# A chunked state-space scan feeding a cosine-gated two-layer network: the scan cut into twelve 64-token units instead of six 128-token chunks

## The chip, the core and the metric

One core of a Trainium2 chip runs the whole program. The metric is the device time of one execution in microseconds (us). The kernel before was timed in three runs. One further execution was recorded by the hardware profiler, and all rows below come from that one. The engines are TensorE (PE in the profile, its weight loads PEld), VectorE (DVE), ScalarE (ACT), GpSimd (POOL) and SyncE (SP, which here only issues transfers).

## What is computed

There are two stages. The first is a scan over 768 tokens, for 4 sequences of 8 heads, with a state of 16 by 32 for each head. The second multiplies the 3072 rows of 256 numbers with `w_in`, gates with `h * cos(h)` and multiplies with `w_out`.

```python
# scan: x (4, 8, 768, 32), a (4, 8, 768), B and C (4, 8, 768, 16); chunk = 32
cum = np.cumsum(la, axis=-1)                       # la = log(clip(a)) of one chunk
L = np.exp(cum[:, :, :, None] - cum[:, :, None, :]) * causal
M = np.einsum('bhin,bhjn->bhij', Cc, Bc) * L
y_intra = np.einsum('bhij,bhjd->bhid', M, xc)
y_inter = np.einsum('bhin,bhnd->bhid', Cc, state) * np.exp(cum)[:, :, :, None]
y[:, :, sl] = y_intra + y_inter
Bx = np.einsum('bhjn,bhjd->bhjnd', Bc, xc) * decay_from_j[:, :, :, None, None]
state = decay_full[:, :, None, None] * state + np.sum(Bx, axis=2)
# network on the 3072 x 256 rows: w_in 256 x 2048, w_out 2048 x 256
h = x @ w_in
out = (h * np.cos(h)) @ w_out
```

The chunk length is free, because the recurrence gives the same result for any cut. The weights come as 64-bit numbers and are turned into 32-bit ones on the chip.

## The kernel before

**Steps of the network.** The main loop (lines 827 to 884) has 96 steps, 16 for each of six chunks of 128 tokens. A step takes 256 rows (the tokens of two sequences) and one eighth of the 2048 columns. `first(n)` (line 568) multiplies four times on TensorE into the PSUM tile `hp` (line 578); ScalarE makes the integer turn `k` (line 582), VectorE the remainder `w` (line 584), ScalarE the sine (line 589) and VectorE the gated product `gT` (line 594). `second(n)` runs two steps later on TensorE: four multiplications in the first 16 steps (line 637) and seven smaller ones after that (line 675), for which GpSimd prepares differences `gd` (lines 619 to 622). The order of TensorE in a step is therefore hp of step n, then o of step n-2, then, after some steps, a piece of the scan.

**Weights.** `w_in` and `w_out` arrive in eight pieces each (`fetch`, line 197). Each piece is converted by `grade` (ScalarE line 222 and 220, GpSimd line 223) and `join` (VectorE lines 236 and 238, GpSimd line 246). The dictionary `piece` (line 768) says in which step a piece is joined: at an odd step n piece (n+3)/2 of `w_in`, at an even step n piece n/2 of `w_out`. With `turn_of` (line 563) the steps 2j and 2j+1 of chunk 0 use piece j of both. `join` of step n stands on VectorE between `w` and `gT` of that step.

**Scan of a chunk.** Tokens lie on the 128 partitions, one sequence at a time. `decays` (line 372) makes the decay matrix `lam` with a running product on VectorE (line 378), `intra2` (line 463) multiplies C and B on TensorE in tiles of 32 rows by 64 columns of the array (line 474), `masked` (line 480) multiplies the two on VectorE (line 495), and `finish2` (line 499) adds on TensorE the share of the old state (line 509, tiles of 32 by 64), the share of the chunk itself (line 516, tiles of 128 by 32) and the new state (line 537, same tiles). From chunk 2 on, B and C are also fetched in 32-token blocks (`load_blocks`, line 135), which VectorE transposes (line 438). TensorE visits the scan three times per chunk: `intra2` for sequences 0 and 1, `intra2` for 2 and 3, and `finish2` for all four. PSUM has two buffers of two banks for it (`pair`, line 89).

**Start.** Chunk 0 is computed before step 0, except for sequence 3, whose last part stands after hp of step 0 (`first_scan`, line 786). Two filling multiplications (line 730) keep TensorE going from the start while inputs arrive. Transfers are issued by SP in program order (`load` line 127, `fetch` line 197, and so on); a transfer waits for the eighth transfer before it.

Of the kernel before, what the change touches and what calls it, by code (L numbers as in the profile page):

```python
# [25 lines left out]
def kernel(  # L26
# [10 lines left out]

# [11 lines left out]
    HH = H // 2  # L67
# [3 lines left out]
    W = P // 2  # L71

    const = ctx.enter_context(tc.tile_pool(name="const", bufs=1))
    loads = ctx.enter_context(tc.tile_pool(name="loads", bufs=2))
    rows = ctx.enter_context(tc.tile_pool(name="rows", bufs=NB))
# [4 lines left out]
    two = ctx.enter_context(tc.tile_pool(name="two", bufs=2))  # L80
# [8 lines left out]
    def pair(name):  # L89

        return psum.tile([P, 2, 4 * P], FP32, tag="scan", bufs=2, name=name)


    raw, arow, along, blocks = {}, {}, {}, {}
# [9 lines left out]

# [3 lines left out]
    def load(c, seqs=(0, NB), only=(B, C, x)):  # L108

        if c >= NC:  # L110
            return
        if c not in raw:
            raw[c] = (loads.tile([P, 2, NB * H, N], FP32, tag="bc", name="bc"),
                      loads.tile([P, NB, H, D], FP32, tag="xr", name="xr"))
        bc, xr = raw[c]
        xr = xr.rearrange("p b h d -> p (b h) d")
        for dst, src in ((bc[:, 0], B), (bc[:, 1], C), (xr, x))[::2 if c > 1 else 1]:

            if not any(src is o for o in only):
                continue  # L120
            halves = c > 0 and src is not C
            for b in range(*seqs) if halves else seqs[:1]:
                rs = slice(b * H, (b + 1 if halves else seqs[1]) * H)
                for t in range(2 if halves and b % 2 else 1):
                    n = W if halves and b % 2 else P
                    ts = slice((n - t * W) % P, (n - t * W) % P + n)
                    nc.sync.dma_start(  # L127
                        out=dst[ts, rs], in_=src[b:b + 1 if halves else seqs[1], :,
                                                 c * P + t * W:c * P + t * W + n, :]
                        .rearrange("b h s n -> s (b h) n"))  # L130

    def by_blocks(c, u):
        return c > 1

    def load_blocks(c, u):

        blocks[c, u] = to_ = loads.tile([P, 2, 2, 4, 2, N], FP32, tag="blocks", name="blocks")  # L140
        for s in range(2):
            for k, src in enumerate((B, C)):
                of = src[2 * u + s, :, c * P:(c + 1) * P].rearrange(
                    "(q h) (m t) n -> m h q t n", h=2, t=32)
                for m in range(4):
                    for h in range(2):
                        nc.sync.dma_start(out=to_[:, k, s, (m + 2 * s) % 4 if k == 0 else m, h],
                                          in_=of[m, h])
                        yield

    def load_a(c, seqs=range(NB)):
        if c >= NC:
            return
        for b in seqs:
            arow[c, b] = t = rows.tile([P, H, P], FP32, tag="arow", name="arow")
            nc.sync.dma_start(
                out=t, in_=a_cut[b, :, c * P:(c + 1) * P].unsqueeze(0).to_broadcast([P, H, P]))

    def load_along(c, seqs=range(NB)):

        if c >= NC:
            return
        if c not in along:
            along[c] = rows.tile([P, NB, P], FP32, tag="along", bufs=2, name="along")
        for b in seqs:
            nc.sync.dma_start(
                out=along[c][:, b], in_=a_all[b, :, c * P:(c + 1) * P].unsqueeze(1)
                .to_broadcast([H, N, P]))


    a0 = const.tile([P, P], FP32, name="a0")
    a0z = const.tile([P, P], FP32, name="a0z")
    nc.sync.dma_start(out=a0[0:NB * H], in_=a[:, :, 0:P].rearrange("b h p -> (b h) p"))
    for r in (slice(NB * H, W), slice(W, P)):
        V.memset(a0[r], 1.0)
# [34 lines left out]

# [19 lines left out]
    def join(which, i):  # L230

        parts = held.pop((which, i), ())
        for e, (high, bits, last) in enumerate(parts):
# [12 lines left out]
    for b in range(NB):  # L248
        if b == NB - 1:
            fetch("in", 0)  # L250
        load(0, (b, b + 1))
    nc.sync.dma_start(
        out=a_in, in_=a.rearrange("(u b) h (c p) -> (b h c) u p", u=NU, p=P))
    for w in (("in", 1), ("out", 0), ("in", 2), ("out", 1), ("in", 3)):
        fetch(*w)
# [5 lines left out]
    V.memset(quarter, HALF_PI)  # L261


    unit = const.tile([P, HH * P + W], FP32, name="unit")
    G.tensor_copy(out=unit[:, 0:HH * P].rearrange("p (h i) -> p h i", h=HH),
                  in_=ident.unsqueeze(1).to_broadcast([P, HH, P]))


    ms = [scan.tile([P, 2 * H * W], FP32, tag=f"m{b}", bufs=1, name="m") for b in range(NB)]
    m_of = [t.rearrange("p (e h i) -> p e h i", e=2, h=H) for t in ms]  # L270
    m_at = [t.rearrange("p (h i) -> p h i", h=H) for t in ms]
    unit0, tos = m_of[NB - 1][:, 0], m_of[NB - 1][:, 1]
    for t in range(2):
        ts = slice(t * W, (t + 1) * W)
        V.tensor_copy(out=unit0[ts], in_=ident[ts, ts].unsqueeze(1).to_broadcast([W, H, W]))

    slot = const.tile([P, 2], FP32, name="slot")
    mine = const.tile([P, H], FP32, name="mine")
    those = const.tile([P, NB], FP32, name="those")
    bh = ident[:, 0:NB * H]  # L280
# [5 lines left out]
    ACT.activation(const.tile([P, 1], FP32, name="sine"), quarter, AF.Sin)  # L286


# [3 lines left out]
    V.tensor_scalar(out=a0, in0=a0, **clip)  # L292


    to = const.tile([P, W], FP32, name="to")
    V.tensor_tensor_scan(out=to, data0=a0[:, W:P], data1=ones[:, 0:W], initial=1.0,
                         op0=ALU.mult, op1=ALU.mult)
    fro = const.tile([P, W], FP32, name="fro")
    V.memset(fro, 1.0)
    V.tensor_tensor_scan(out=fro[:, W - 2::-1], data0=a0[:, W - 1:0:-1],  # L300
                         data1=ones[:, 0:W - 1], initial=1.0, op0=ALU.mult, op1=ALU.mult)
    fros = const.tile([P, NB, W], FP32, name="fros")
    V.tensor_tensor(out=fros, in0=fro.unsqueeze(1).to_broadcast([P, NB, W]),
                    in1=those.unsqueeze(2).to_broadcast([P, NB, W]), op=ALU.mult)
    V.tensor_reduce(out=slot, in_=ident.rearrange("p (k t n) -> p t k n", t=2, n=N),
                    axis=mybir.AxisListType.XY, op=ALU.add)


    a0s = m_of[NB - 2]
    halves = a0z.rearrange("p (t i) -> p t i", t=2)  # L310
    for h in range(HH):
        ACT.activation(a0s[:, :, h], halves, AF.Copy, scale=mine[:, h:h + 1])
# [5 lines left out]


    scaled, lam, reach, state, part, yT = {}, {}, {}, {}, {}, {}  # L320

    def heads(b):
        return slice(b * H, (b + 1) * H)

# [104 lines left out]

    turned = {}

    def turn_blocks(c, u):
# [479 lines left out]
```

## Time and profile before

| what | value |
|---|---|
| median of three runs | 377.41 us |
| lowest and highest | 376.71 and 377.42 us |
| span of the profiled execution, first to last instruction | 374.9 us |
| busy: TensorE, VectorE, GpSimd, ScalarE | 367.1, 286.0, 215.1, 176.0 us |
| matmul records on TensorE | 3108 |
| start of hp of step 0, 1 and 2 | 17.81, 21.16 and 23.32 us |
| start of the first o (step 0's second product) | 25.71 us |
| end of the last o | 371.2 us |
| spacing of hp and of o, first 16 steps | 1.73 and 1.73 us |
| spacing of hp and of o, later steps | 1.73 and 1.56 us |

The span leaves out 2.5 us of the median. The profiled execution has no time of its own besides the span. A multiplication of 32-bit numbers appears as two matmul records with a weight load each. TensorE's records overlap and their ends are modelled, so the spacing from one start to the next is read, not the duration. A line of the timeline gives start, duration, engine, source line, operation, destination and source tile, shape and count, and in brackets the idle time before it and what ended it.

### The profile page before, as it was taken

The page shows a single profiled execution, that of the slowest core. Times are in us where ns is not written, and L with a number is a line of the kernel's source. Part 1 is how long each engine was busy: PE and PEld are TensorE (multiplying, and loading weights), DVE is VectorE, ACT ScalarE, POOL GpSimd, SP SyncE. Part 2 cuts the span into 40 slices and gives each one's busy share as a digit, 9 for nine tenths or more (in the row PEclk, how much of TensorE's full clock was granted, in tenths as well). Part 3 has the DMA queues.
Part 4 walks back from the last instruction along what each step waited for, and adds up shares of the span by engine and source line. Part 5 has one row for each costly group of instructions (what it writes and reads, how often), then busy time and mean ns, then how long its engine had stood idle before and what let it go on. Part 6 is the DMA issues. An engine that isn't in the chain of part 4 may idle for free.

```text
span 374.9 us, 8382 instructions
## 1 busy us (share of the span) xinstructions
PE 367.1 (98%) x3108; PEld 325.4 (87%) x3108; DVE 286.0 (76%) x478; ACT 176.0 (47%) x304; POOL 215.1 (57%) x335
## 2 busy tenths in 40 slices
PE   8999999999999999999999999999999999999996
PEld 3478888889899899999899998999999989999995
DVE  8879999889799957987767987766887872554543
ACT  3887666544344434344334445434444443443442
POOL 6767555589946346665354693353775344444451
PEclk9999999999999999999999999999999999999999
DMA  7989896514545741663322655121020000010011
GB/s 84 263 239 285 243 219 117 128 15 99 151 92 78 131 108 16 84 153 77 76 54 21 91 141 131 25 51 17 4 41 8 11 21 2 0 30 0 2 28 29
DMA packets 124424, 31.52 MB, mean 84 GB/s; under 512 B 93568, under 2 KB 120288, under 8 KB 124384
## 3 DMA queue, kind: packets, MB, share of 16 engines
q1 hardware_dynamic: 124224, 30.86, 38.4%
q8 instruction: 24, 0.39, 0.4%
q14 instruction: 16, 0.13, 0.1%
q10 hardware_dynamic: 160, 0.13, 0.1%
HBM read 27.64 MB, written 3.34 MB: 83 GB/s over the span
## 4 chain that ended last, share of the span: by engine, by line
PE 83%; SPq 5%; POOL 4%; DMA 3%; DVE 2%; issue 1%; ACT 1%; POOLq 0%; DVEq 0%; ACTq 0%
PE hp L578 40%; PE o L675 29%; PE o L637 7%; SPq L127 4%; PE y L516 3%; PE g L474 2%; DMA words<-in_moe_w_in_dram 1%; POOL words L613 1%; PE y L509 1%; POOL gd L619 1%; DMA bc<-in_B_dram 1%; DMA blocks<-in_C_dram 1%; POOL gd L622 1%; PE o L720 1%; PE s_ps L537 0%
## 5 line engine op out<-in xcount | busy, mean ns | idle before, releaser
L578 PE MATMUL hp<-yT,w_in 128*128 128x256 f32 x768 | 183.7, 382 | 1.9 <-DVE gT L594 1.4
L578 PEld LDWEIGHTS hp<-yT,w_in 128*128 128x128 f32 x768 | 139.4, 190 | 21.6 <-issue 2.0
L619 POOL TENSOR_TENSOR gd<-gT 128x256 f32<-128x256 f32 x79 | 59.2, 750 | 100.0 <-DVE gT L594 91.2
L589 ACT ACTIVATE w<-w,quarter 128x512 f32<-128x512 f32 x96 | 69.2, 721 | 76.8 <-DVE w L584 76.7
L582 ACT ACTIVATE k<-hp 128x512 int32<-128x512 f32 x96 | 57.2, 595 | 82.3 <-PE hp L578 82.0
L584 DVE SCALAR_TENSOR_TENSOR w<-hp,k 128x512 f32<-128x512 f32 x96 | 65.4, 681 | 37.3 <-ACT k L582 37.1
L594 DVE TENSOR_TENSOR gT<-hp,w 128x512 f32<-128x512 f32 x96 | 65.2, 679 | 34.6 <-ACT w L589 24.8
L675 PE MATMUL o<-words,gd 128*128 128x128 f32 x474 | 65.9, 275 | 0.0
L675 PEld LDWEIGHTS o<-words,gd 128*128 128x128 f32 x474 | 59.3, 192 | 0.1
L378 DVE TENSOR_TENSOR_SCAN lam<-arow,unit 128x512 f32<-128x512 f32 x40 | 57.0, 1426 | 0.0
L675 PEld LDWEIGHTS o<-w_out,gT 128*128 128x128 f32 x316 | 47.5, 191 | 4.0
L622 POOL TENSOR_TENSOR gd<-gT,gd 128x128 f32<-128x128 f32 x79 | 45.5, 577 | 6.2
L675 PE MATMUL o<-w_out,gT 128*128 128x128 f32 x316 | 48.0, 274 | 0.0
L621 POOL TENSOR_TENSOR gd<-gT,gd 128x128 f32<-128x128 f32 x79 | 44.2, 560 | 6.2
L495 DVE TENSOR_TENSOR m<-g,lam 128x256 f32<-128x256 f32 x80 | 30.9, 415 | 0.5
L637 PE MATMUL o<-w_out,gT 128*128 128x256 f32 x128 | 30.3, 380 | 0.4 <-POOL w_out L246 0.4
L675 PE MATMUL o<-w_out,gd 128*128 128x128 f32 x158 | 30.6, 275 | 0.0
L675 PE MATMUL o<-words,gT 128*128 128x128 f32 x158 | 30.6, 275 | 0.0
L637 PEld LDWEIGHTS o<-w_out,gT 128*128 128x128 f32 x128 | 24.2, 190 | 4.0 <-POOL w_out L246 0.8
L675 PEld LDWEIGHTS o<-words,gT 128*128 128x128 f32 x158 | 24.0, 192 | 0.0
L675 PEld LDWEIGHTS o<-w_out,gd 128*128 128x128 f32 x158 | 24.0, 192 | 0.0
L692 DVE TENSOR_TENSOR sum<-ps,sum 128x256 f32<-128x256 f32 (+1 forms) x27 | 16.7, 644 | 0.6
(98 smaller groups left out, 274.5 us busy)
## 6 DMA issues: line engine op xcount, KB each, us to landing
arow<-a_cut SPq DMA_DIRECT2D x20, 512.0 KB
words<-in_moe_w_in_dram SPq DMA_DIRECT2D x8, 512.0 KB
words<-in_moe_w_out_dram SPq DMA_DIRECT2D x8, 512.0 KB
out_dram<-sum SPq DMA_DIRECT2D x18, 128.0 KB
blocks<-in_B_dram SPq DMA_DIRECT2D x128, 8.0 KB
blocks<-in_C_dram SPq DMA_DIRECT2D x128, 8.0 KB
xr<-in_x_dram SPq DMA_DIRECT2D x14, 128.0 KB
along<-a_all SPq DMA_DIRECT2D x20, 64.0 KB
```

Source lines behind the costliest of these rows:

```text
L378: V.tensor_tensor_scan(out=lam[c, b][:, hs].rearrange("p h i -> p (h i)"), data0=rows_.rearrange("p h i -> p (h i)"), data1=unit[:, b % 2 ...
L495: V.tensor_tensor(out=m_[js, :, :, is_], in0=g_[js, :, :, is_], in1=l_[js, :, :, is_], op=ALU.mult)
L578: PE.matmul(to_[:, e], lhsT=w_in[:, k, fs], rhs=y[:, k, u], start=(k == 0), stop=(k == KT - 1), skip_group_check=True)
L582: ACT.activation(k, hp[n], AF.Copy, bias=0.25, scale=INV_2PI)
L584: V.scalar_tensor_tensor(out=w, in0=hp[n], scalar=INV_2PI, in1=k, op0=ALU.mult, op1=ALU.subtract)
L589: ACT.activation(cos, cos, AF.Sin, bias=quarter, scale=TWO_PI)
L594: V.tensor_tensor(out=gT[n], in0=hp.pop(n), in1=cos, op=ALU.mult)
L619: G.tensor_tensor(out=d[:, 0:2], in0=g[:, 1:2].to_broadcast([P, 2, P]), in1=g[:, 3::-3], op=ALU.subtract)
L621: G.tensor_tensor(out=d[:, 2], in0=g[:, 0], in1=d[:, 0], op=ALU.subtract)
L622: G.tensor_tensor(out=d[:, 3], in0=g[:, 2], in1=d[:, 2], op=ALU.subtract)
L637: PE.matmul(o[c, u][:, t], lhsT=g[:, 2 * e + t], rhs=w_out[:, 2 * j + e], start=(j == e == t == 0), stop=(j == NJ - 1 and e == 1), skip_gr ...
L675: PE.matmul(at[q], lhsT=a_[q], rhs=w[q], start=(j == 0 and q in starts), stop=(j == NJ - 1), skip_group_check=True)
```

## The change

The scan works in twelve units of 64 tokens. Two sequences share the 128 partitions: partitions 0 to 63 hold sequence p, 64 to 127 sequence 2+p, for p of 0 and 1. A decay matrix is 64 by 64 for each head, and `decays` runs twice per unit. TensorE does one visit per unit, in one PSUM buffer of four banks: `inner` of unit k (C times B) and then `outer` of unit k-1 (old state, own share, new state). All its matmuls have 64 or 128 columns. `yT` and the new state are copied out by VectorE, the state's decay is applied by GpSimd.

Unit 0 is done before step 0. A step still takes 256 rows and one eighth of the columns, but the rows are now one unit of all four sequences, so unit k has the eight steps 8k to 8k+7. For the first 16 steps the order is different: steps 0 and 1 are pieces 0 and 1 of unit 0, steps 2 and 3 the same of unit 1, and from step 4 on even steps belong to unit 0 and odd ones to unit 1. Unit 1 is turned after hp of step 0, its `inner` stands after hp of step 1, and its `outer` ahead of hp of step 2. The step in which a weight piece is joined changes with it, and SP's order of transfers too; four of the first transfers are issued by ScalarE's queue. One filling multiplication is left out of two.

```diff
-    def pair(name):
-        return psum.tile([P, 2, 4 * P], FP32, tag="scan", bufs=2, name=name)
+    def whole(name):
+        return psum.tile([P, 4, 4 * P], FP32, tag="scan", bufs=1, name=name)
...
+    load_bc(0, (1,), nc.scalar)
+    load_bc(0, (0,))
+    fetch("in", 0)
+    load_x(0, nc.scalar)
+    fetch("in", 1)
+    load_bc(1)
+    fetch("out", 0)
+    load_x(1)
+    load_along(1)
+    fetch("out", 1)
...
+    def inner(k, g):
+        g_of[k] = g
+        bT, cT = turned[k][:, 0], cut_.pop(k)
+        for p in range(2):
+            for s in range(2):
+                ss = slice(s * W, (s + 1) * W)
                 for q in range(4):
                     r = slice(32 * q, 32 * q + 32)
+                    PE.matmul(g[ss, q, p * P:(p + 1) * P].rearrange("p (t i) -> p t i", t=2),
+                              lhsT=bT[r, p, ss], rhs=cT[r, p, :, ss], start=True, stop=True,
+                              tile_position=(32 * q, s * W), skip_group_check=True)
+
+    def weights(k, p):
...
+        V.tensor_tensor(out=m_of[k][:, p].rearrange("p (q t) i -> p q (t i)", t=2),
+                        in0=g_of[k][:, :, p * P:(p + 1) * P],
+                        in1=lam[k][:, p].rearrange("p (q t) i -> p q (t i)", t=2), op=ALU.mult)
+
+    def outer(k, ps):
...
+                    for h in range(H):
+                        r, q = slice(32 * (h // 2), 32 * (h // 2) + 32), h % 4
+                        PE.matmul(ps[32 * q:32 * q + 32, 2 * (h // 4) + s,
+                                     2 * P + p * W:2 * P + (p + 1) * W],
+                                  lhsT=state[k][r, s, p, h % 2 * D:(h % 2 + 1) * D],
+                                  rhs=r_[r, p, s * W:(s + 1) * W], start=(p == 0), stop=False,
+                                  tile_position=(32 * (h // 2), 32 * q), skip_group_check=True)
...
+                    for q in range(4):
+                        PE.matmul(ps[32 * q:32 * q + 32, 2 * t + s,
+                                     2 * P + p * W:2 * P + (p + 1) * W],
+                                  lhsT=xk[ss, p, 4 * t + q], rhs=m[ss, p, 4 * t + q],
+                                  start=(k == p == 0), stop=True,
+                                  tile_position=(s * W, 32 * q), skip_group_check=True)
...
+                    for q in range(4):
+                        PE.matmul(ps[32 * q:32 * q + 32, s, 3 * P + p * W:3 * P + (p + 1) * W],
+                                  lhsT=sc[ss, p, q], rhs=x2[ss, p, q], start=False,
+                                  stop=True, tile_position=(s * W, 32 * q), skip_group_check=True)
+        yT[k] = two.tile([P, 2, 2 * P], FP32, tag="yT", name="yT")
+        V.tensor_copy(out=yT[k].rearrange("p t (s i) -> p (t s) i", s=2), in_=ps[:, :, 2 * P:3 * P])
...
     def turn_of(n):
-        c, f = divmod(n, NF)
-        return (f % 2, f // 2) if c == 0 else divmod(f, NJ)
+        if n >= NF:
+            return divmod(n, NJ)
+        return divmod(n, 2) if n < 4 else (n % 2, n // 2)
...
+    fill(bank([P, 4, P], "warm", "o"), 1)
+    for p in range(2):
+        spread_a(0, p)
+    decays(0, 0)
+    turn_first([bank([P, 2, P], "tp", "o") for _ in range(2)])
+    decays(0, 1)
+    weigh(0)
+    spread_a(1, 0)
     grade("in", 0, n=2)
+    decays(1, 0)
+    spread_a(1, 1)
+    visit(0, None)
+    for p in (1, 0):
+        weights(0, p)
+    join("in", 0, (0,))
+    visit(None, 0)
+    join("in", 0, (1,))
     grade("in", 1)
+    decays(1, 1)
+    weigh(1)
+    join("in", 1)
     rest = grade("out", 0, later=True)
...
-    piece = {n: ("in", (n + 3) // 2) if n % 2 else ("out", n // 2) for n in range(NF)}
+    piece = {0: ("out", 0), 2: ("out", 1), 3: ("in", 2)}
+    for j in range(2, NJ):
+        piece[2 * j + 1] = ("out", j)
+        if j < NJ - 1:
+            piece[2 * j] = ("in", j + 1)
+    piece[2 * NJ - 2] = piece.pop(2 * NJ - 1)
...
+    at(after, 0, lambda: turn(1, bank([P, 4, P], "tp", "o")))
...
+    at(behind, 0, reaches, 1)
+    at(behind, 1, weigh_c, 1)
+    at(visits, 1, visit, 1, None)
+    for p in (1, 0):
+        at(visits, 1, weights, 1, p)
+    at(ahead, 2, visit, None, 1)
+    at(visits, 4, visit_turn, 2)
...
+    at(visits, 6, visit, 2, None)
...
+    at(visits, 10, visit_turn, 3)
+    for k in range(3, NK):
+        f = k * NJ
...
+        at(behind, f - 11, decays, k, 0)
+        at(visits, f - 11, visit, k, k - 1)
+        at(behind, f - 9, decays, k, 1)
...
+        for p in (1, 0):
+            at(behind, f - 8, weights, k, p)
+    at(visits, NT - 11, visit, None, NK - 1)
```

`visit(k, l)` takes the four-bank buffer and calls `inner(k, ...)` and `outer(l, ...)`, where None leaves one out; `visit_turn` transposes B and C of a unit there. In a step the lists are served in this order: `ahead` before hp, `after` behind hp, `behind` around `gT` on VectorE, `visits` behind the o of the step. `reaches` is the running product along the tokens, `weigh_c` multiplies it into C, and `weigh` multiplies B with the last row of the decay matrices.

## The prediction

> **What bounds it.** I read the page first, busy times and the 40 slices, then the chain of waits, then the timeline around the first step, a scan visit and an early step, and last the clock. All numbers are us unless said otherwise.
>
> ```profile
> PE 367.1 (98%) x3108; PEld 325.4 (87%) x3108; DVE 286.0 (76%) x478; ACT 176.0 (47%) x304; POOL 215.1 (57%) x335
> PE   8999999999999999999999999999999999999996
> DVE  8879999889799957987767987766887872554543
> PE 83%; SPq 5%; POOL 4%; DMA 3%; DVE 2%; issue 1%; ACT 1%; POOLq 0%; DVEq 0%; ACTq 0%
> ```
>
> TensorE is full in every slice but the ends, and has most of the chain. So the time is TensorE's start, its work and its waits. VectorE is nearly full only in the first third: what is late there stalls TensorE.
>
> ```profile
> 17.81 2.29 PE L578 MATMUL hp<-yT,w_in 128*128 128x256 f32 x8 [0.33 <-POOL w_in L246]
> ...
> 25.71 1.99 PE L637 MATMUL o<-w_out,gT 128*128 128x256 f32 x8 [0.42 <-POOL w_out L246]
> ```
>
> I call the start of the first o X: 25.71 here. From X on the network itself needs 93 hp of 1.73, 16 o of 1.73, 79 o of 1.56, a last o of 1.99 and a tail of 3.7 (from 371.2 to 374.9): 317.3. The remaining 374.9 - 25.7 - 317.3 = 31.9 are scan visits and their stalls.
>
> ```profile
> 169.35 0.64 PEld L474 LDWEIGHTS g<-cT,turned 32*64 32x64 f32 x32
> 169.36 0.91 PE L474 MATMUL g<-cT,turned 32*64 32x256 f32 x32
> ...
> 170.19 1.99 PE L578 MATMUL hp<-yT,w_in 128*128 128x256 f32 x8
> ```
> ```profile
> 132.69 1.10 PE L509 MATMUL y<-rT,state 32*64 32x128 f32 x32
> ...
> 133.72 1.96 PE L516 MATMUL y<-m,xr 128*32 128x128 f32 x64
> ...
> 135.50 0.63 PE L537 MATMUL s_ps<-xr,sc 128*32 128x64 f32 x32
> ...
> 136.06 1.99 PE L578 MATMUL hp<-yT,w_in 128*128 128x256 f32 x8
> ```
>
> **Scan work on TensorE.** A clean chunk costs two g visits (0.84 each to the next hp, plus 0.19 by which the o before and the hp behind are longer) and one finish (136.06 - 132.69 = 3.37, plus 0.19): 5.6. Array time: L537 runs four 64-column tiles side by side, 32 records in 0.45 (13.9 ns each), so one such tile is 0.111 per matmul (two records); L509 gives 0.218 for 128 columns. L474 keeps eight tiles busy at once: its tiles have 384 columns each, three times 0.218 = 0.65, and the visit costs 1.03, so entering and leaving cost 0.38.
>
> After: inner is 16 matmuls on eight tiles, 2 x 0.218 = 0.44; old state and own share are 32 each on eight tiles, 4 x 0.111 = 0.445 each; new state 0.22. Two changes of tile shape at 0.13 (L509 to L516 is 0.20 from start to start, where groups follow at 0.09) and the 0.38 make 2.2 per visit. Its records are twice as many per token; if no more than one per 13.9 ns can start, 192 of them take 2.67 and the visit 3.3. The lower bound is 1.9, without the shape changes. I take 2.2, because L474 is the row with eight tiles. The Trainium skill, "TensorE: Matmul & The Clock Gate", "Wait — 56ns, not 53.3ns?", says start to start never falls below about 25 ns. By that 192 records would take 4.8 and nine visits 19 more than by the row of 13.9. The row contradicts it where tiles alternate.
>
> From X on there are: two turns at 0.53 (as L452, 0.44 + 0.09), inner of unit 2 alone 0.8, nine visits 19.8, the last outer 1.4: 23.1. The stalls of before at late blocks and gates (some 3.5 in the 31.9) go, if SP keeps up: it issues 88 transfers per 16 steps instead of 84 at about 0.56, 49 of 57 us; the blocks have two steps of slack. VectorE's scan work per 16 steps falls (eight running products of 1.43 become four), hidden under TensorE in both. The copy of yT (0.67) goes from ScalarE to VectorE, between gT and the next w, which waits for hp anyway. The four PSUM banks are one buffer: VectorE reads them for the last time three steps after a visit, and the next visit comes after eight. If these masks were five steps late, TensorE would wait for them.
>
> **Weights joined late.** This is new, and on the path.
>
> ```profile
> 30.99 1.89 PE L578 MATMUL hp<-yT,w_in 128*128 128x256 f32 x8
> ...
> 32.98 0.60 ACT L582 ACTIVATE k<-hp 128x512 int32<-128x512 f32 x1 [0.21 <-PE hp L578]
> ...
> 33.61 0.69 DVE L584 SCALAR_TENSOR_TENSOR w<-hp,k 128x512 f32<-128x512 f32 x1 [0.23 <-ACT k L582]
> ...
> 34.22 0.42 DVE L236 TENSOR_SCALAR mag<-mag 128x512 uint32<-128x512 uint32 x1
> ...
> 34.67 0.98 DVE L238 SCALAR_TENSOR_TENSOR mag<-words,mag 128x512 uint32<-128x512 uint32 x1
> ...
> 35.73 1.27 POOL L246 TENSOR_TENSOR w_out<-mag,last 128x512 uint32<-128x512 uint32 x1 [0.62 <-DVE mag L238]
> ```
>
> A piece joined in step n is ready 4.3 after that hp's end (32.72 to 37.00). Before, an o piece has two steps. After, `w_out` piece j from 2 on is joined in step 2j+1 and used by the o behind hp of step 2j+2: 3.46 later. TensorE waits 0.9, for pieces 1 (joined in step 2) to 5; piece 6 is covered by the visit of step 13. `w_in` piece 2, joined in step 3 and used by hp of step 4, has only one o (1.73) between, itself 0.9 late: 1.7 more. Sum 5 x 0.9 + 1.7 = 6.2. Bounds 4 (L238 at 0.69, as at 39.03) and 8 (ready 4.9 after hp, as in step 5, where a running product stood in front of w).
>
> **The start.** VectorE sets it. Spread matmuls begin at about 4.5 (4.77 before), the first running product at 5.7. Three products at 1.21, two masks at 0.65: about 11. Own share and new state 0.7, copy of yT 0.67: hp 0 starts near 13.5, 4 earlier than now. Its second half waits for the second share of `w_in` piece 0 (VectorE 0.8, GpSimd 0.73, queued behind the copies) and ends near 16.3. Behind it VectorE has a product 1.21 and the join 1.3, GpSimd 1.28: hp 1 at 19. Now unit 1: VectorE needs k, w, then the sine, which stands on ScalarE behind a copy 0.59 and two cuts at 0.45, gT 0.68 ending at 20.4; join of `w_out` piece 0 1.3; running product of 260 about 0.8; w 0.68; sine 0.72; gT 0.68 ending at 24.6; masks 1.3: 25.9. Only then outer of unit 1, 1.6, yT 0.67, and hp 2 at 28.5 against 23.32 now. X is 30. Bounds 28.5 and 31: seventeen VectorE pieces stand in this chain, and the same pieces differ by up to 0.3 (L238 is 0.69 or 0.98). hp 2 waits on TensorE with o 0, hp 3 and everything else queued behind it, so its 5 us are lost whole.
>
> What is not on this chain: transfers before the first weights are seven of 64 or 128 KB at 0.7 to 1.0 each, so piece 0 lands near 9 (12.0 now) and is needed at 11; later than that, hp 0 goes with it. GpSimd's clips of `a` wait for a transfer of about 19, with the join of `w_out` piece 0 queued behind them, due at 30. SP waits near 26 for `a_all` before the rows of unit 2, with `w_out` piece 2 behind it; some 8 later that piece has landed, and step 4 grades it at about 40.
>
> **The clock adds to it.** The groups by shape have the same 128x512 matmul at two speeds (the last number before the second bar is the mean in ns), and the table by stretches shows the granted clock (third column from the end):
>
> ```profile
> L101 PE MATMUL warm<-ones 128*128 128x512 f32 x4 | 3.8, 1101 | 1.1 <-DVE ones L96 1.1
> L351 PE MATMUL l_ps<-m,fros 128*128 128x512 f32 x4 | 2.0, 594 | 0.0
> ```
> ```profile
> 373.00:374.00 1.00, 0.00 (x0) 0.00 (x0) 0.00 (x0) 0.00 (x0) 0.00 (x0) 0.79 0.42 105
> 374.00:374.90 0.90, 0.00 (x0) 0.00 (x0) 0.00 (x0) 0.00 (x0) 0.00 (x0) 0.50 0.00 0
> ```
>
> TensorE became fast some 3.8 after its first matmul (1.06; the rows at 4.77 are the first fast ones), kept busy by two fills; and 2.4 after its last o (371.2) the clock falls from 1 to 0.5, at about 373.6. With one fill it rests from 2.8 to 4.5: the spreads may run at half speed until about 8.3, 1.7 later on the chain (bounds 0 and 2.5). From inner of unit 1 (ending 21.5) to 26 it rests 4.5, longer than 2.4: 3.8 at half speed lose 1.9 (bound 0). I take 3.5 for both: X 33.5.
>
> **Sum.** 33.5 + 317.3 + 23.1 + 6.2 = 380.1 of span against 374.9. The median stands 2.5 over the span: 382.6. X must be below 28.3 for a gain.
>
> **Rivals.** (1) Small matmuls start no faster than 13.9 ns each: visits of 3.3 add 10, the other pieces 2.5: 395. For it the tiny tiles, against it L474. (2) Faster: unit 1 doesn't hold hp 2 back, its chain on VectorE ending with hp 1 at 20.7; inner, outer and hp 2 (0.8 + 1.7 + 1.7) put X at 25 and the clock stays up: 25 + 346.6 + 2.5 = 374.1. For it: hp 0 really starts 4 earlier; against it the serial sum on VectorE. It decides at X = 28.3. (3) SP falls behind in the later units, as the g visit at 124.40 with 1.55 instead of 0.84 shows for one chunk: eight units at 0.7 add 5.6: 388.
>
> **Numbers.** Forecast 0.57, rival 1 0.13, rival 2 0.15, rival 3 0.10, sums cancelling 0.05. Own range of the forecast 377.5 (no cold clock, stalls 4.5) to 388. The whole range 376.5 to 391 leaves out most of rivals 1 and 2. 0.2% is 0.75, about what a measurement here can tell from no change: faster 0.15, same 0.05, slower 0.80.
>
> **What would show it.** hp 0 starting before 15 and hp 2 after 27; gaps of about 0.9 ahead of every second o in steps 3 to 10, ended by GpSimd's join; visits of 2.2 in the rows of inner and outer; half-speed rows of outer and hp 2 near 27. Wrong: hp 2 before 25, or no gap ahead of these o.

## The result, and the profile after

The changed kernel takes 402.74 us (median of 4 runs, 400.42 to 404.80) against 377.39 before: 1.0673 times as long (95% interval 1.0625 to 1.0721). The forecast said slower, which is right, but 382.6 with a range to 391, which is far off. All numbers below are us unless said otherwise. The profiled execution has a span of 399.6.

The page of the changed kernel (busy time, then the slices of TensorE, then the chain that ended last):

```profile
PE 372.8 (93%) x4252; PEld 329.9 (83%) x4252; DVE 249.6 (62%) x383; ACT 167.0 (42%) x277; POOL 207.1 (52%) x341
PE   8747799899989999998999999999999999999995
PE 71%; SPq 10%; DVE 6%; issue 4%; DMA 3%; ACT 3%; POOL 2%; DVEq 0%; ACTq 0%; POOLq 0%
```

TensorE has 1144 records more than before and is now idle in slices that were full: the second to the fifth, and a little in many later ones. The share "issue" of the chain has grown from 1% to 4% (16 us): time in which an engine waited for nothing that the profile shows.

The timeline of TensorE at the start (start, duration, line; the last bracket is the idle time before and what ended it):

```profile
3.79 3.68 PE L285 MATMUL a_ps<-a0s,those 32*64 32x512 f32 x8 [0.66 <-POOL a0s L256]
...
17.02 3.48 PE L450 MATMUL hp<-yT,w_in 128*128 128x256 f32 x8 [0.88 <-DVE yT L407]
...
22.38 1.99 PE L450 MATMUL hp<-yT,w_in 128*128 128x256 f32 x8 [1.45 <-POOL w_in L212]
...
29.14 0.84 PE L381 MATMUL ps<-rT,state 32*32 32x64 f32 x64 [4.15 <-DVE m L368]
...
32.73 0.47 PE L403 MATMUL ps<-xr,sc 64*32 64x64 f32 x16 [1.52 <-issue]
34.03 3.47 PE L450 MATMUL hp<-yT,w_in 128*128 128x256 f32 x8 [0.84 <-DVE yT L407]
37.34 1.89 PE L508 MATMUL o<-w_out,gT 128*128 128x256 f32 x8
```

hp 0 starts at 17.02, hp 1 at 22.38, hp 2 at 34.03, the first o (X) at 37.34. hp 2 takes 3.47 where hp 1 took 1.99. The table by stretches of two us (granted clock third from the end) says why:

```profile
28.00:30.00 2.00, 0.85 (x72) 0.79 (x80) 1.00 (x2) 0.00 (x0) 0.29 (x1) 1.00 0.19 55
30.00:32.00 2.00, 1.21 (x80) 0.97 (x81) 0.00 (x0) 0.00 (x0) 0.00 (x0) 0.56 0.26 57
...
34.00:36.00 2.00, 1.97 (x5) 1.61 (x6) 0.31 (x1) 0.00 (x0) 0.72 (x1) 0.50 0.94 186
36.00:38.00 2.00, 2.00 (x9) 1.69 (x8) 0.00 (x0) 0.46 (x1) 0.00 (x0) 0.74 1.07 298
```

The clock is at half speed from 30.2 to 37.1. And one visit of a later unit, then another:

```profile
115.23 0.69 PE L360 MATMUL ps<-cT,turned 32*64 32x128 f32 x32
115.85 0.91 PE L381 MATMUL ps<-rT,state 32*32 32x64 f32 x64
116.69 1.13 PE L391 MATMUL ps<-m,xr 64*32 64x64 f32 x61
...
119.22 0.44 PE L403 MATMUL ps<-xr,sc 64*32 64x64 f32 x26 [1.29 <-issue]
```
```profile
208.64 0.69 PE L360 MATMUL ps<-cT,turned 32*64 32x128 f32 x32
209.27 0.87 PE L381 MATMUL ps<-rT,state 32*32 32x64 f32 x64
210.07 0.90 PE L391 MATMUL ps<-m,xr 64*32 64x64 f32 x60
...
211.50 1.99 PE L450 MATMUL hp<-yT,w_in 128*128 128x256 f32 x8
```

The first stands still for 1.29 in the middle of the new state's matmuls; the second doesn't. To count what each costs, take the start of the o ahead and the start of the hp behind and subtract the o's own 1.56 (1.73 in the first 16 steps): 4.46 for the first, 2.95 for the second. So the miss divides (0.2 of it are rounding):

| term | forecast | measured | miss |
|---|---|---|---|
| first o (X) | 33.5 | 37.34 | +3.8 |
| nine visits: 2.79, 4.46, 4.74, 4.96, 2.95, 3.03, 3.21, 3.08, 2.60 | 19.8 | 31.82 | +12.0 |
| of these, standing still inside (1.29, 1.56, 1.80) | 0 | 4.65 | |
| two turns, inner of unit 2, the last outer | 3.3 | 3.46 | +0.2 |
| weights joined late: 0.81, 1.72, 0.93, 0.82, 0.87, 0.82 | 6.2 | 5.97 | -0.2 |
| a wait of 0.54 at 264.8 and what is under 0.12 each | 0 | 2.1 | +2.1 |
| tail behind the start of the last o (1.99 + 3.7 forecast) | 5.7 | 7.04 | +1.4 |
| span | 380.1 | 399.6 | +19.5 |
| median over the span | 2.5 | 3.1 | +0.6 |

### The profile page after: what moved, and what is told of

The parts are those of the page before. It is cut to its first block, busy times and chain, and to the rows that moved or that the text cites. A ratio compares the mean times of both kernels' runs of the same rounds, so it can differ in the third digit from the quotient of the medians.

```text
span 399.6 us, 10534 instructions
## 1 busy us (share of the span) xinstructions
PE 372.8 (93%) x4252; PEld 329.9 (83%) x4252; DVE 249.6 (62%) x383; ACT 167.0 (42%) x277; POOL 207.1 (52%) x341
## 4 chain that ended last, share of the span: by engine, by line
PE 71%; SPq 10%; DVE 6%; issue 4%; DMA 3%; ACT 3%; POOL 2%; DVEq 0%; ACTq 0%; POOLq 0%
PE hp L450 34%; PE o L546 25%; PE o L508 5%; SPq L120 4%; SPq L98 3%; PE ps L391 2%; PE ps L381 2%; SPq L136 1%; PE ps L360 1%; PE ps L403 1%; POOL w_out L212 1%; DVE mag L204 1%; DMA bc<-in_B_dram 1%; DVE w L456 1%; DVE sum L563 1%
## 5 line engine op out<-in xcount | busy, mean ns | idle before, releaser
L450 PE MATMUL hp<-yT,w_in 128*128 128x256 f32 x768 | 186.3, 386 | 5.0 <-POOL w_in L212 2.9
L450 PEld LDWEIGHTS hp<-yT,w_in 128*128 128x128 f32 x768 | 141.3, 193 | 23.9 <-POOL w_in L212 4.0
L491 POOL TENSOR_TENSOR gd<-gT 128x256 f32<-128x256 f32 x79 | 58.0, 734 | 118.5 <-DVE gT L466 100.7
L494 POOL TENSOR_TENSOR gd<-gT,gd 128x128 f32<-128x128 f32 x79 | 38.5, 488 | 6.2
L493 POOL TENSOR_TENSOR gd<-gT,gd 128x128 f32<-128x128 f32 x79 | 37.9, 479 | 6.2
L295 DVE TENSOR_TENSOR_SCAN lam<-arow,unit 128x512 f32<-128x512 f32 x20 | 28.9, 1447 | 0.0
L189 POOL TENSOR_SCALAR mag<-mag 128x512 f32<-128x512 f32 (+1 forms) x17 | 12.8, 752 | 17.0 <-ACT mag L188 16.9
L407 DVE COPY yT<-ps 128x512 f32<-128x512 f32 x12 | 8.3, 689 | 21.1 <-PE ps L403 20.9
```

Source lines behind the costliest of these rows:

```text
L295: V.tensor_tensor_scan(out=lam[k][:, p].rearrange(flat), data0=rows_.rearrange(flat), data1=unit.rearrange(flat), initial=0.0, op0=ALU.mul ...
L450: PE.matmul(to_[:, e], lhsT=w_in[:, t, fs], rhs=yT[k][:, t], start=(t == 0), stop=(t == KT - 1), skip_group_check=True)
L491: G.tensor_tensor(out=d[:, 0:2], in0=g[:, 1:2].to_broadcast([P, 2, P]), in1=g[:, 3::-3], op=ALU.subtract)
L493: G.tensor_tensor(out=d[:, 2], in0=g[:, 0], in1=d[:, 0], op=ALU.subtract)
L494: G.tensor_tensor(out=d[:, 3], in0=g[:, 2], in1=d[:, 2], op=ALU.subtract)
```

## The experiments

Each was compared with the kernel before on its own chip, so the ratios are what can be compared: 1.0673 for the changed kernel. A difference of 0.0027 between two ratios is 1 us; the intervals of two ratios together leave each such difference open by 2 to 3 us.

### Early joins

```
-    piece = {0: ("out", 0), 2: ("out", 1), 3: ("in", 2)}
+    piece = {0: ("out", 0), 2: ("out", 1)}
     for j in range(2, NJ):
-        piece[2 * j + 1] = ("out", j)
+        piece[2 * j] = ("out", j)
         if j < NJ - 1:
-            piece[2 * j] = ("in", j + 1)
-    piece[2 * NJ - 2] = piece.pop(2 * NJ - 1)
+            piece[2 * j - 1] = ("in", j + 1)
...
+    at(behind, 2, grade, "in", 2)
+    at(behind, 2, join, "in", 2)
```

> From step 3 on each piece of w_out is joined in step 2j instead of 2j+1, and each piece of w_in one step earlier too (piece 2 at the end of step 2). Theory A (weights joined late cost what was forecast): the six gaps ahead of o behind hp 3, 6, 8, 10, 12 and ahead of hp 4, 5.97 together in the trace of the changed kernel, go, and no new one comes; the time falls by 5 to 6.5. Rival (VectorE and GpSimd are late there whatever the schedule): gaps of the same size stand ahead of other steps, and the time falls by less than 2.

398.93, ratio 1.0593 (1.0551 to 1.0635), span 399.2: by the ratios some 3 of the time, half of what theory A said. The timeline of the profiled execution shows 3.7 gained at the joins and 3.5 lost again. The four gaps behind hp 6 to hp 12 are gone (3.44 of the 5.97), while the two around hp 4, whose piece is joined in step 2 in both kernels or just after, stay with 0.80 and 1.45. But this run lost 3.5 in two places that the schedule doesn't touch. Around the first, its hp 22, by stretches:

```profile
115.00:116.00 1.00, 0.33 (x26) 0.28 (x26) 0.00 (x0) 0.00 (x0) 0.92 (x4) 1.00 0.15 14
116.00:117.00 1.00, 1.00 (x16) 0.79 (x4) 0.80 (x2) 0.00 (x0) 0.28 (x1) 0.64 0.17 16
117.00:118.00 1.00, 1.00 (x4) 0.82 (x3) 0.23 (x1) 0.00 (x0) 0.63 (x1) 0.50 0.20 29
```

Behind a visit that stood still for 1.31, TensorE was at half speed from 116.28 to 119.69, and behind one that stood still for 1.76 again from 181.13 to 184.55. hp 22 took 3.58. So the gaps were the joins', as theory A says; the gain is less because two gaps stay, and standing still can cost a second time through the clock.

### Split visits

```
-        at(visits, f - 11, visit, k, k - 1)
+        at(visits, f - 11, visit, None, k - 1, True)
+        at(visits, f - 10, visit2, k, k - 1)
```

The first of the two issues old state and own share of k - 1 with the copy of yT, the second inner of k and the new state of k - 1. The outer of unit 1 is cut in the same way, its new state behind the first o.

> The visit is cut in two: old state and own share (256 records of the trace: 128 matmuls and 128 weight loads) in their gap, inner and the new state (128 records) one step later; the first hp of unit 1 no longer has the new state ahead of it. Theory B (TensorE's instructions come in pieces of 16 KB, one piece is some 253 records, the next is not there until about 3.4 after the last was begun, and a visit of 384 records in 2.6 to 3.2 runs out of them): the idle stretches of 1.3 to 1.8 marked issue in the visits at 117.9, 148.9 and 180.2 and in the outer of unit 1 at 31.2 all go, 6.2 together, and no other of over 0.8 comes; nine further entries into small tiles cost about 0.4 each; the time falls by 2 to 4. Rival (the stretches are a wait for something else, late data or a semaphore): they stay, or move with the new state's matmuls, and the time rises by 3 to 5.

396.88, ratio 1.0539 (1.0510 to 1.0567), span 394.5. One unit's visit in this run:

```profile
115.63 0.85 PE L381 MATMUL ps<-rT,state 32*32 32x64 f32 x64
116.41 0.86 PE L391 MATMUL ps<-m,xr 64*32 64x64 f32 x64
117.20 1.99 PE L468 MATMUL hp<-yT,w_in 128*128 128x256 f32 x8
...
120.69 0.69 PE L360 MATMUL ps<-cT,turned 32*64 32x128 f32 x32
121.31 0.45 PE L411 MATMUL ps<-xr,sc 64*32 64x64 f32 x32
121.70 1.56 PE L468 MATMUL hp<-yT,w_in 128*128 128x256 f32 x6
```

No visit stands still any more. The gain of 5 is above the 2 to 4 expected, because the second entry costs nothing: the two parts together are 1.67 + 1.10 to 1.91 + 1.18, or 2.77 to 3.1, as much as a whole undisturbed visit. The same data are needed at nearly the same times, so the rival falls. Only hp 4 waits longer than in the changed kernel, 2.54 instead of 1.72.

### Shifted records

```
+    def pad():
+        t = whole("pad")
+        for i in range(27):
+            r, q = slice(32 * (i % 4), 32 * (i % 4) + 32), i // 4 % 4
+            PE.matmul(t[32 * q:32 * q + 32, i % 4, 0:W], lhsT=ident[r, 0:32], rhs=ident[r, 0:W],
...
+    at(visits, 17, pad)
```

> The changed kernel with 27 further small matmuls (108 records) in a gap of step 17, writing banks that nothing reads. In the changed kernel the idle stretches marked issue stand after record 332, 357 and 382 of the visits at 115.2, 146.1 and 177.3, 25 later in each unit, and the later visits have none. Theory B (a new 16 KB piece of instructions begins every 253 to 254 records, and a visit that uses up a whole piece runs dry): everything moves 108 records ahead, so the stretches stand after about record 274, 299, 324, 349 and 374 of the third to seventh visit after the insertion (those at 177, 208, 238, 268 and 298, plus what was added), the first has none, the second may have a short one near 249, and the time rises by 2 to 6. Rival (what is late is data of units 4 to 6): the stretches stay in the same three visits, and the time rises by the 1 to 1.5 of the added matmuls.

404.03, ratio 1.0731 (1.0701 to 1.0762): some 2 more, which alone would not tell theory B from its rival. The places do tell them apart. Counting the matmul and weight-load records in each visit up to the stretch: in the changed kernel 332, 357, 382 in the third to fifth whole visit (the first is that of unit 1, at 24.3) and none later; here none in those three, then 300, 325, 350, 375 in the four that follow, and none in the last (in the hp right behind that one a wait of 0.30 marked issue). The forecast positions were 299, 324, 349, 374. The one forecast at 274 (and the short one at 249) did not come. In the chain of waits the first of them:

```profile
206.56 0.85 PE ps L381 x56
207.40 1.01 PE ps L391 x40
208.41 0.86 issue
209.27 0.27 PE ps L391 x5
```

The data of the visits are the same; only the count of records ahead is another, and the stretches move with it. So what is late is TensorE's own instructions. The pages agree in amount: their rows for the DMA queue that carries instructions, the changed kernel first, then the one before:

```profile
q8 instruction: 33, 0.54, 0.6%
```
```profile
q8 instruction: 24, 0.39, 0.4%
```

33 packets and 0.54 MB for 2 x 4252 records, 24 and 0.39 MB for 2 x 3108: some 63 B a record and 16 KB a packet. The packets' times in the changed kernel's trace, beside the four places where TensorE stood still:

```
packet starts   packet ends   TensorE goes on   from its end
 30.12           31.37          32.73            1.36
116.90          117.82         119.22            1.40
147.61          149.06         150.48            1.42
179.24          180.56         181.96            1.40
```

Each time TensorE goes on 1.36 to 1.42 after a packet has ended; in the other five traces with such stretches (early joins, shifted records, half the columns, warm start, unit 1 off the start) it is 1.17 to 1.62. The stretches move 25 records per unit of 736, so three pieces are 761 and one is 253.7 records. The Trainium skill, "Runtime: NRT & Kernel Launch", "Instruction fetch mechanics", has the pieces of 16 KiB too, and says that crossing into one is mostly hidden. Mostly it is here too: of the 33 packets four made TensorE stand still. Where a piece begins late in a visit of 384 records it isn't, and there the measurement decides.

### Half the columns

```
-                                     2 * P + p * W:2 * P + (p + 1) * W],
+                                     2 * P + p * W:2 * P + p * W + 32],
...
-                                  rhs=r_[r, p, s * W:(s + 1) * W], start=(p == 0), stop=False,
+                                  rhs=r_[r, p, s * W:s * W + 32], start=(p == 0), stop=False,
...
+                        lo_ = 32 if k > 0 else 0
...
-                                     2 * P + p * W:2 * P + (p + 1) * W],
-                                  lhsT=xk[ss, p, 4 * t + q], rhs=m[ss, p, 4 * t + q],
+                                     2 * P + p * W + lo_:2 * P + (p + 1) * W],
+                                  lhsT=xk[ss, p, 4 * t + q], rhs=m[ss, p, 4 * t + q, lo_:],
```

> From unit 1 on the old state's matmuls go over the first 32 tokens of each 64 and the own share's over the last 32, so that half of each sum is left out; number and order of instructions are the same, the columns of each are half. Theory D (small matmuls are bound by the number of records, some 10 to 12 ns each, not by their columns): the two groups keep 0.64 to 0.95 each from first start to last, the clean visits 2.6 to 3.2, the time falls by less than 1. Rival (the columns set it): each group falls by 0.2 to 0.4, the visits by 0.5 to 0.7, and the time by 5 to 7.

404.01, ratio 1.0748 (1.0695 to 1.0800). The same groups with half the columns (x32 in the shape where x64 stood):

```profile
269.59 0.85 PE L381 MATMUL ps<-rT,state 32*32 32x32 f32 x64
270.37 1.14 PE L392 MATMUL ps<-m,xr 64*32 64x32 f32 x61
```

Undisturbed visits cost 2.69, 2.98, 3.03, 3.13, 3.12 and 2.40, against 2.79, 2.95, 3.03, 3.21, 3.08 and 2.60. Halving the columns does not shorten them by the 0.5 to 0.7 that array time would give; the last moves most, by 0.2. The time is no shorter either (3.4 at half speed behind one visit are in this profile). So the columns do not set the time of these groups. That the number of records does is what is left of the two, and it fits the matmuls added in the run before (54 records of 64 columns cost 0.79 there); the number was not varied by itself. Whether the matmul or its weight load sets the pace was not tried.

### A warm start

```
-    fill(bank([P, 4, P], "warm", "o"), 1)
+    fill(bank([P, 4, P], "warm", "o"), 2)
...
     visit(0, None)
+    fill(bank([P, 4, P], "warm", "o"), 2)
...
+    at(ahead, 2, lambda: fill(bank([P, 4, P], "warm", "o"), 4))
     at(ahead, 2, visit, None, 1)
```

> Two fills at the start instead of one, two more fills behind inner of unit 0 and four ahead of the outer of unit 1, all while TensorE has nothing else. Theory C (the cold clock is what makes hp 0 and hp 2 late beyond the forecast): the spreads run at 0.43 each instead of 0.85, hp 0 starts at 13.5 to 14.5 instead of 17.0, hp 2 takes 1.9 instead of 3.47 and starts at 29.5 to 31.5 instead of 34.0, the first o is at 31 to 33.5 and the time falls by 4 to 6. Rival (VectorE's chain and the transfers hold the start, not the clock): hp 0 stays later than 16, and only hp 2 itself gets shorter; the time falls by 1 to 2.

404.23, ratio 1.0728 (1.0701 to 1.0755): no gain at all.

```profile
13.33 1.10 PE L450 MATMUL hp<-yT,w_in 128*128 128x256 f32 x4 [0.88 <-DVE yT L407]
...
27.34 0.97 PE L381 MATMUL ps<-rT,state 32*32 32x64 f32 x64 [2.23 <-DVE m L368]
...
31.54 0.67 PE L403 MATMUL ps<-xr,sc 64*32 64x64 f32 x30 [2.03 <-issue]
33.05 3.36 PE L450 MATMUL hp<-yT,w_in 128*128 128x256 f32 x7 [0.83 <-DVE yT L407]
```

The clock is at full speed from 3.98, and hp 0 starts at 13.33 as theory C says. But nothing of it reaches X (36.6): outer of unit 1, 1.8 earlier than in the changed kernel, stands still for 2.03; the fills end at 25, the clock falls at 27.87, and hp 2 is slow again. And with 28 records more ahead, the later visits stand still at 304, 329, 354 and 379, four instead of three, two of them with 3.4 at half speed behind.

### Unit 1 taken off the start

```
-                PE.matmul(to_[:, e], lhsT=w_in[:, t, fs], rhs=yT[k][:, t],
+                PE.matmul(to_[:, e], lhsT=w_in[:, t, fs], rhs=yT[0 if n < 4 else k][:, t],
...
-    at(ahead, 2, visit, None, 1)
-    at(visits, 4, visit_turn, 2)
+    at(ahead, 4, visit, None, 1)
+    at(visits, 5, visit_turn, 2)
```

> The changed kernel, but steps 2 and 3 take the scan's result of unit 0 again instead of that of unit 1 (their share of the output is left out so), and the outer of unit 1 stands ahead of step 4. All instructions are the same. Theory E (the serial chain of unit 1 on VectorE, with TensorE idle behind it and the clock that falls in that rest, is what makes the first o late): hp 2 starts within 1 of inner of unit 1, near 25, at full speed; the first o is at 26.5 to 28 instead of 37.3; hp 4 still has to wait for the outer of unit 1 and for the joins, but the time falls by 5 to 9. Rival (VectorE's load as a whole is what is late, not that chain): hp 4 starts where it did, at 44 to 46, and the time falls by less than 2.

395.28, ratio 1.0468 (1.0439 to 1.0498), some 8 less:

```profile
24.34 0.69 PE L360 MATMUL ps<-cT,turned 32*64 32x128 f32 x32
24.96 1.99 PE L450 MATMUL hp<-yT,w_in 128*128 128x256 f32 x8
27.28 1.99 PE L508 MATMUL o<-w_out,gT 128*128 128x256 f32 x8 [0.32 <-POOL w_out L212]
...
36.29 1.99 PE L450 MATMUL hp<-yT,w_in 128*128 128x256 f32 x8
```

hp 2 at 24.96, X at 27.28, hp 4 at 36.29 against 45.06: all as theory E says. The clock, at full speed from 21.3, does not fall: TensorE no longer rests for 4.15, and no rest above 1.5 is left. The outer of unit 1 does not stand still either. So the serial chain of unit 1 costs X ten us, with the clock and the missing instructions that come with it here, and some of that comes back at later joins.

### All parts together, and two variants

All parts: the early joins, split visits, a warm start with seven fills ahead of outer of unit 1, and in the last step (the variants are shown against this run):

```
-                of = whole("o").rearrange("p b (q m) -> p b q m", m=P)
-                lo, hi = of[:, 0], of[:, 1]
-                mid = bank([P, 4, P], "o", "o")
+                lo = whole("o").rearrange("p b (q m) -> p b q m", m=P)[:, 0]
+                mid, hi = (bank([P, 4, P], "o", "o") for _ in range(2))
```

> Early joins, split visits, two fills at the start, two behind inner of unit 0, seven ahead of the outer of unit 1, and a bank of its own for the second accumulator of the last step. By the parts: hp 2 near 29.5 and the first o near 31 to 32 with the clock at full speed from 5 on; no gap ahead of an o or hp in steps 3 to 12, no stretch marked issue over 0.8 in a visit, no clock at 0.5 behind one; visits of 2.8 to 3.0 in two parts; the tail 1.4 shorter. Theory (the miss is these terms and nothing else): 379 to 383 of span, 381.5 to 385.5 in time, still slower than the kernel before by 1 to 2%. Rival (parts of these terms give way to another wait): 387 or more.

391.44, ratio 1.0392 (1.0362 to 1.0422), span 388.5: the time is the rival's. From X on most parts do what was said: no visit stands still, the clock never falls, 352.2 from X to the end, in which the nine visits take 26.2 (2.76 to 3.03 each). The joins around hp 4 still cost 0.36 and 1.46, and the tail is 6.15, 0.9 shorter and not 1.4. In the changed kernel the second accumulator's matmuls waited for VectorE's read of the first, which lies in the same buffer; with its own bank the eight records run through:

```profile
392.56 1.13 PE L591 MATMUL o<-w_out,gT 128*128 128x256 f32 x4
...
394.34 1.13 PE L591 MATMUL o<-w_out,gT 128*128 128x256 f32 x4 [0.65 <-DVE ob L594]
```
```profile
382.38 1.99 PE L608 MATMUL o<-w_out,gT 128*128 128x256 f32 x8
```

The start missed: X at 36.3, not 31 to 32. The clock rose at 5.24 and fell at 8.66 for two windows, hp 0 came at 17.17 again, and the seven fills, cut for an earlier start, ran to 31.9 when the masks of unit 1 had been ready since 29.3.

The first variant places the fills anew.

```
+    fill(bank([P, 4, P], "warm", "o"), 1)
     decays(0, 0)
     turn_first([bank([P, 2, P], "tp", "o") for _ in range(2)])
+    fill(whole("warm")[:, 0].rearrange("p (q m) -> p q m", m=P), 1)
...
     at(after, 0, lambda: turn(1, bank([P, 4, P], "tp", "o")))
+    at(after, 0, lambda: fill(bank([P, 4, P], "warm", "o"), 2))
...
-    at(ahead, 2, lambda: fill(bank([P, 4, P], "warm", "o"), 7))
+    at(ahead, 2, lambda: fill(bank([P, 4, P], "warm", "o"), 4))
-    rest = grade("out", 0, later=True)
+            rests = [grade("out", 0, later=True)] if n == 0 else []
```

> As the run with all parts, with the fills placed anew: two at the start, one behind the spreads of unit 0, one behind its turn, two behind inner of unit 0, two behind the turn of unit 1, four instead of seven ahead of its outer; and k of step 0 stands ahead of the grading of the first piece of w_out on ScalarE. Theory (the start is held by the cold clock first and by the chain of unit 1 then): the clock stays at full speed from about 5 on, hp 0 starts near 13.5, hp 1 near 18.7, the masks of unit 1 end near 25.5, hp 2 starts at 27.5 to 29 and the first o is at 29.5 to 31; the rest of the span stays at 352 as in that run: 381.5 to 383.5, the time 384 to 387. Rival (the start is bound by the arrival of rows and weights): hp 0 or hp 1 stay within 1 of 17.2 and 22.5, and the time is 389 or more.

390.36, ratio 1.0336 (1.0298 to 1.0375), span 389.5: the time is the rival's, but its reason, that transfers hold the start, is not what the rows show.

```profile
4.76 3.68 PE L285 MATMUL a_ps<-a0s,those 32*64 32x512 f32 x8
8.37 2.08 PE L86 MATMUL warm<-ones 128*128 128x512 f32 x2
...
11.09 1.91 PE L86 MATMUL warm<-ones 128*128 128x512 f32 x2
```

The two fills at the start did not raise the clock this time (it rose at 13.19), so the added fills ran at half speed, 1.9 each, in front of the work: hp 0 at 19.40, X at 37.04. The rest is 352.5 again.

The second variant gives unit 0 the first four steps and unit 1 the next four:

```
-        return divmod(n, 2) if n < 4 else (n % 2, n // 2)
+        return divmod(n, 4) if n < 8 else (n % 2, n // 2)
...
+    piece = {0: [("in", 2), ("out", 0)], 1: [("in", 3), ("out", 1)], 4: [("out", 2), ("out", 3)],
...
-    at(ahead, 2, visit, None, 1, True)
+    at(ahead, 4, visit, None, 1, True)
```

The first four pieces of both weights are fetched ahead of most rows of unit 1.

> As the last, but unit 0 is used for the first four steps and unit 1 for the next four, so that the scan of unit 1 is due ahead of step 4 instead of step 2; the first four pieces of both weights are loaded and joined earlier, and the rows of unit 1 later. Theory E (unit 1's serial chain on VectorE is what holds the start, with hp 2 as its place): the first o comes at 22 to 25, hp 4 at 31 to 34 against 37 to 38 in the last kernel, and the time is 375 to 381. Rival (weights and rows cannot arrive or be joined in time): hp 2 or hp 3 wait for GpSimd's join or a transfer, hp 4 is at 36 or later, and the time is 382 or more.

398.32, ratio 1.0573 (1.0544 to 1.0603): the rival holds.

```profile
41.72 0.88 PE L383 MATMUL ps<-rT,state 32*32 32x64 f32 x64 [2.45 <-DVE m L370]
...
44.53 3.65 PE L470 MATMUL hp<-yT,w_in 128*128 128x256 f32 x8 [1.03 <-DVE yT L402]
52.28 3.78 PE L528 MATMUL o<-w_out,gT 128*128 128x256 f32 x8 [4.11 <-POOL w_out L212]
```

The first o comes at 32 and not at 22 to 25, with the clock cold until 17.2 and hp 0 at 19.55. The outer of unit 1 still waits 2.45 for its masks, hp 4 comes at 44.5 and at half speed, and the o behind it at 52.3 after 4.11 for a piece of `w_out`: the longest wait moves from unit 1's chain to a join.

## Why the prediction was wrong

**The start of X: mechanism right, sizes off by 3.8.** hp 2 does wait for unit 1's chain on VectorE, and taking that chain away brings X to 27.28. The sign "hp 0 starting before 15" did not come: hp 0 is at 17.02, where the sum has 13.5 and 1.7 for the cold clock, so 1.8 of the 3.8 were lost by then. The step that failed there is "the spreads may run at half speed until about 8.3": TensorE was at half speed until 19.99, so that inner of unit 0 ended late and its masks began at 13.1, where the working has them at some 9.7 (1.3 long and ending at 11).

```profile
13.12 1.29 DVE L368 TENSOR_TENSOR m<-ps,lam 128x512 f32<-128x512 f32 x2 [1.44 <-PE ps L360]
```

With the clock up, in the warm start, hp 0 is at 13.33 (13.5 without the cold clock in the working) and hp 1 at 18.70 (19). The forecast bounded the loss at 2.5 because it took one warm-up of 3.8 for granted. The half speed at hp 2 was foreseen, at 1.9; there it was from 30.2 to 37.1 and came on top of 1.52 of missing instructions. The other 0.5 is a balance of small differences.

**The visits: the step that failed first.** "old state and own share are 32 each on eight tiles, 4 x 0.111 = 0.445 each" took array time, scaled by columns. In the undisturbed visits the groups take 0.64 to 0.95 from first to last start, and half the columns leave them at 0.56 to 0.99. The records start every 10 to 15 ns. Rival 1 had this mechanism, priced at 13.9; its visit of 3.3 is above the 2.6 to 3.2 of the undisturbed ones, and the 25 ns from start to start that the prediction quoted from the Trainium skill ("TensorE: Matmul & The Clock Gate", "Wait — 56ns, not 53.3ns?") are contradicted by every undisturbed visit, 192 matmul records in at most 3.2. The reason for choosing 2.2, that the row L474 has eight tiles, was weak: L474 has 128 or 256 columns per record, and its records start some 20 ns apart (32 in 0.61), so that it could not show what records of 64 columns cost. The choice cost 9 x 0.82 = 7.4.

**Missing instructions: not in the prediction at all.** 4.65 in three visits, 1.52 ahead of hp 2. The page of before showed the queue (0.39 MB of instructions); the records of a visit were counted as TensorE time and never as something to be fetched.

**Late weights: right.** Six gaps, 5.97 against 6.2, at the steps named, ended by GpSimd's join. The one ahead of hp 4 and the one behind hp 6:

```profile
45.06 1.99 PE L450 MATMUL hp<-yT,w_in 128*128 128x256 f32 x8 [1.46 <-POOL w_in L212]
...
55.18 1.99 PE L508 MATMUL o<-w_out,gT 128*128 128x256 f32 x8 [0.77 <-POOL w_out L212]
```

**The tail: overlooked.** 1.4, for which the sum has no term. 0.9 of it come from two accumulators in one buffer and go when each has its own. The other 0.5 stand behind VectorE's last addition (3.68 to the end of the span, 3.21 before), are still there with all parts, and were not explained.

**SP (rival 3): nearly nothing.** SyncE's share of the chain is larger, but on TensorE there is only one later wait of any size, 0.54 at 264.8, ended by VectorE. Why the g visit at 124.40 in the kernel before was long, from which that rival was drawn, was not tried.

**Rival 2** needed that unit 1 does not hold hp 2, and it does. Where it doesn't, with unit 1 taken off the start, X is under 28.3 as that rival said, but the gain doesn't follow: with X at 27.28 the span is 391.1.

No version beats the kernel before. The best, 390.36, takes 352.5 from X on, the kernel before 374.9 - 25.7 = 349.2. So the scan in units of 64 is not cheaper on TensorE even when nothing stands still: nine visits of 2.9, turns and the rest come to some 32, as the scan and stalls of before did (31.9); the joins around hp 4 and the tail are the rest of the 3, and the start is 11 later. Whether a start with the clock up from 4 to the end and split visits would reach X near 30 stays open: in the two runs built for it the clock was at half speed until 13.2 or again from 8.7 to 15.5.

## What to carry to other kernels

Count a change's small matmuls as records, at the pace of rows with as few columns per record, and count them a second time as instructions to be fetched: a dense burst of more records than one piece should be cut and spread over the steps. Ahead of the first large matmul, ask for each stretch what keeps TensorE's clock up, and do not rely on fills that last 3.4 to 3.8, as these did. A chain of a dozen serial pieces on VectorE ahead of the second unit's first use holds TensorE, and the clock falls while it rests.

## What the runs showed of the hardware

- TensorE's instructions come in packets of 16 KB, one per 253.7 matmul and load records, and a stretch without them lasts 0.7 to 2.0 in these traces. In a visit of 384 dense records one came when a new piece began after record 300 to 382, none at 274. The positions are the same in each profiled run with the same count of records ahead (332, 357, 382 in three of them; 331, 356, 381 with unit 1 taken off the start).
- The clock changes in steps of 3.413 (each stretch at half speed in these traces, but the one cut off by the end of the kernel, is 3.41, 6.83 or 10.24 long). The Trainium skill, "TensorE: Matmul & The Clock Gate", "Part 1: The HAM clock gate (the "warmup" mystery)", gives the same 3413 ns, free-running. Its advice in "HAM oscillation — how this bites in real kernels", no idle gap over some 3.4, was not enough here: five times a visit that stood still for 0.7 to 1.8 was followed by 3.41 at half speed (early joins two, warm start two, half the columns one), and at other times the same stretch was not. What decides stays open. The share of busy time in a window does not: if the windows are laid out in steps of 3.413 from the recorded changes, TensorE was busy 2.62 of the one that ended in the fall at 120.32 with half the columns, and 2.37 of the one from 115.56 in the changed kernel, which ended in none.
- Work on TensorE without a pause does not always keep the clock up: with all parts it fell at 8.66, after 3.42 in which TensorE was busy throughout with spreads of 32 x 64, transposes and the start of inner. That small tiles do not count as work is not shown: by the same layout of windows the changed kernel has two with nothing else, busy 2.37 (from 115.56) and 2.64 (from 146.28), and the clock stayed up behind both. Two fills (3.4 to 3.8 long) were followed by full speed within 0.5 in three profiled runs (the kernel before, the warm start, all parts) and not in two (the two variants).
- The clock in the table by stretches is 1.00 until the first change is recorded, even where the matmuls run at half speed (the spreads at 3.79: eight records in 3.68, and 2.15 in the run with all parts). Durations tell it; that column doesn't.
